# Every load of a decode kernel issued as two: even partitions from SyncE, odd partitions from ScalarE

## The chip, the core and the metric

The kernel runs on one core of a Trainium2 chip. A core has a matrix engine (TensorE, PE in the profile), VectorE (DVE), ScalarE (ACT), GpSimd (POOL) and SyncE (SP), each with its own instruction stream, and 16 DMA engines that move data between the device's memory (HBM) and the on-chip buffer (SBUF, 128 partitions). A load is issued by an instruction on SyncE or ScalarE and signals a semaphore when it has landed. The metric is the device time of the program in microseconds (us), lower is better. Before the change three runs took 219.29, 219.30 and 219.37 us, median 219.3.

## The reference

One decode step for a batch of 2: attention with 32 query heads over the last 4096 positions of a cache with 8 key/value heads, beside a dense layer with the Mish activation, mixed by a gate.

```python
# A: B=2, D=512, Hq=32, Hkv=8, Sk=32768, Dh=128; W=4096
q = (x @ wq).reshape(B, 1, Hq, Dh).transpose(0, 2, 1, 3)
k, v = the last W positions of the caches, each of 8 heads repeated 4 times
p = softmax(einsum("bhqd,bhkd->bhqk", q, k) * Dh ** -0.5)
a = einsum("bhqk,bhkd->bhqd", p, v)  ->  (B, 1, Hq * Dh) @ wo
# B: F=1792
h = x @ w1 + b1
b = (h * tanh(softplus(h))) @ w2
# gate
g = sigmoid((x * gate_w).sum(-1))
return g * a + (1 - g) * b
```

All of it is float32. The weights and the 4096 positions of both caches have to be read once: 91 MB.

## The kernel before, in words

The host lays the inputs out so that each load fills 128 partitions with long contiguous rows. There are three large buffers of 64 KB per partition (pool `stream`, `bufs=3`), and all large loads go through them in this order: `wq` (one piece of 1 MB, one of 7 MB), the caches of key/value heads 0 to 7 (`kv0` to `kv7`, 8 MB each, keys and values of one head side by side), `w12` (w1, the first heads' part of wo and the first seven row blocks of w2, 6.4 MB), `wo` (pieces of 5 MB and 2 MB), and last three pieces of w2 (1 MB, 0.5 MB, 0.25 MB), which go into the free end of `w12`'s buffer. A small load `sm` (13 KB: x, the gate's weights, b1) follows `wq`. All of them are issued by SyncE (`load`, line 64, and lines 70 and 294). A load into a buffer waits until TensorE has finished reading what was in it, so at most three large loads are held at once.

The compute follows the loads. `gates` and `queries` (lines 105 to 140) work from `sm` and `wq`. Then, for each key/value head, `scores` (line 148) multiplies the keys, VectorE finds the maximum (151), ScalarE takes the exponential with its sum (153, the tile `p`), `turned` transposes it on TensorE (160) and ScalarE copies that out (161, `pT`), and `values` multiplies by the values (172, the tile `o`). After every second head VectorE collects the diagonal blocks into `od` (179 to 182). For head 7 the common maximum of all heads and the factors that follow from it (`tops`, `factors`, `shares`) are woven in between. Then come `hidden` (line 235, the tile `hp`, and the Mish chain), `outputs` (224, the tile `ol`), the projection with wo and the first part of w2 (305, the tile `acc`), and the rest of w2 (315, the tile `fin`). A copy and a store end the program; before the store SyncE waits for the last eight loads to have landed (line 343).

The order within an engine is the order in which the scheduler of the language puts the instructions; `pin` keeps the pinned ones in the order written. The scheduler also gives each load one of eight semaphores in turn, and adds a wait to a load whose semaphore still belongs to an earlier load, so that this load goes only when the earlier one has landed. An engine that waits at an instruction does nothing that stands behind it.

Of the kernel before, what the change touches and what calls it, by code (L numbers as in the profile page):

```python
# [9 lines left out]
AF = mybir.ActivationFunctionType  # L10
# [3 lines left out]
P = 128  # L14
B = 2
D = 512
HQ = 32
HKV = 8
REP = HQ // HKV
# [4 lines left out]
BN = B * NH  # L24
NJ = 4
NT = 4
Q = 32
# [3 lines left out]
DC = D // P  # L31
FC = F // P
FG = 4
HALF = 4
CHUNK = 8192
# [4 lines left out]
CUTS = (0, 7, 11, 13, 14)  # L40
WO = (1, 6, 8)
ROWS = (24, 104)
WIDE = 2 * Q - B
AHEAD = DC * F + WO[0] * REP * D
# [3 lines left out]
def decode_kernel(ctx: ExitStack, tc: tile.TileContext, res, stored, small, wqh, wqt, kv_in, w12, wo, w2, out):  # L48
    nc = tc.nc
# [5 lines left out]
    ps_s = ctx.enter_context(tc.tile_pool(name="ps_s", bufs=2, space=bass.MemoryType.PSUM))  # L55
    ps_1 = ctx.enter_context(tc.tile_pool(name="ps_1", bufs=1, space=bass.MemoryType.PSUM))

    loads = []

    def load(name, *parts):  # L60
        t = stream.tile([P, 2 * CHUNK], F32, tag="s", name=name)
        x = 0
        for cols, src in parts:
            loads.append(nc.sync.dma_start(t[:, x : x + cols], src))  # L64
            x += cols
        return t

    wq_t = load("wq", (HEAD, wqh), (2 * CHUNK - HEAD, wqt))
    sm = const.tile([P, SMALL], F32, name="sm")
    loads.append(nc.sync.dma_start(sm, small))  # L70
    xT = sm[:, : DC * B].rearrange("p (c b) -> p c b", b=B)
    gw = sm[:, DC * B : DC * B + DC]
    b1 = sm[:, DC * B + DC :]
# [16 lines left out]
    x32 = const.tile([P, DC, Q], F32, name="x32")  # L90
    nc.gpsimd.memset(x32, 0.0)
    nc.gpsimd.tensor_copy(x32[:, :, ::RS], xT)  # L92
    qz = const.tile([P, HKV, BN * (Q + REP)], F32, name="qz")
# [13 lines left out]
    def gates():  # L107
        xg = const.tile([P, DC, B], F32, name="xg")
        nc.gpsimd.tensor_tensor(xg, xT, gw[:, :, None].to_broadcast([P, DC, B]), op=ALU.mult)
        zp = ps_1.tile([P, B], F32, tag="q", name="zp")  # L110
        for c in range(DC):
            nc.tensor.matmul(zp, ones, xg[:, c, :], start=(c == 0), stop=(c == DC - 1))  # L112
        g = const.tile([P, B], F32, name="g")
        omg = const.tile([P, B], F32, name="omg")
        nc.scalar.activation(g, zp, AF.Exp, scale=-1.0)
        nc.gpsimd.tensor_scalar_add(g, g, 1.0)  # L116
        nc.vector.reciprocal(g, g)  # L117
        nc.gpsimd.tensor_scalar(omg, g, -1.0, 1.0, op0=ALU.mult, op1=ALU.add)
        return g, omg
# [19 lines left out]
        for n in range(NH):  # L139
            nc.vector.tensor_copy(half[:, n], heads)  # L140

    pin = tc.keep_in_program_order

    def scores(kv, t):
        sc = ps_s.tile([P, 512], F32, tag="sc", name=f"sc{kv}")
        for m in range(BN):
            for j in range(NJ):
                nc.tensor.matmul(sc[Q * j : Q * j + Q, :], qz[:, kv, m * Q : m * Q + Q],  # L148
                                 t[:, (m * NJ + j) * 512 : (m * NJ + j + 1) * 512],
                                 start=(m == 0), stop=(m == BN - 1))  # L150
        nc.vector.tensor_reduce(mx[:, kv : kv + 1], sc, axis=AX.X, op=ALU.max, negate=True)  # L151
        p = work.tile([P, 512], F32, tag="p", name=f"p{kv}")
        nc.scalar.activation(p, sc, AF.Exp, bias=mx[:, kv : kv + 1], accum_out=ls[:, kv : kv + 1])  # L153
        return p

    def turned(kv, p):
        pp = ps_1.tile([P, NT, P], F32, tag="pt", name=f"pp{kv}")
        pT = single.tile([P, NT, P], F32, tag="pT", name=f"pT{kv}")
        for c in range(NT):
            pin(nc.tensor.transpose(pp[:, c, :], p[:, c * P : (c + 1) * P], ident))  # L160
        nc.scalar.copy(pT, pp)  # L161
        return pT

    pair = [None]
# [20 lines left out]
    def tops():  # L185
        mt = ps_1.tile([HKV, NJ, Q], F32, tag="q", name="mt")
        pin(nc.tensor.transpose(mt.rearrange("k j r -> k (j r)"), mx, ident))
        ms = const.tile([HKV, NJ, Q], F32, name="ms")
        nc.scalar.copy(ms, mt)
        m4 = ms.rearrange("k j (y n h) -> k j y n h", n=NH, h=REP)  # L190
        mj = const.tile([HKV, NJ, Q // NH // REP, REP], F32, name="mj")
        nc.vector.tensor_tensor(mj, m4[:, :, :, 0, :], m4[:, :, :, 1, :], op=ALU.min)
        top = const.tile([HKV, Q // NH // REP, REP], F32, name="top")
        nc.vector.tensor_reduce(top, mj.rearrange("k j y h -> k y h j"), axis=AX.X, op=ALU.min)  # L194
        for n in range(NH):
            nc.gpsimd.tensor_tensor(m4[:, :, :, n, :], m4[:, :, :, n, :],  # L196
                                    top[:, None].to_broadcast(mj.shape), op=ALU.subtract)
        nc.scalar.activation(ms, ms, AF.Exp, scale=-1.0)
        return ms

    def factors(ms):
# [27 lines left out]
    def hidden(t):  # L229
        w = t[:, : DC * F].rearrange("p (c f) -> p c f", c=DC)  # L230
        hp = ps_s.tile([P, FG * P], F32, tag="sc", name="hp")
        for c in range(DC):
            for j in range(NJ):
                n = min(FG, FC - j * FG) * P
                nc.tensor.matmul(hp[Q * j : Q * j + Q, :n], x32[:, c, :],  # L235
                                 w[:, c, j * FG * P : j * FG * P + n],
                                 start=(c == 0), stop=(c == DC - 1))
        hs = work.tile([P, FG * P], F32, tag="p", name="hs")
        nl = (FC - (NJ - 1) * FG) * P
        nc.scalar.copy(hs[:, :nl], hp[:, :nl])  # L240
        nc.scalar.copy(hs[: Q * (NJ - 1), nl:], hp[: Q * (NJ - 1), nl:])
        ht = ps_1.tile([P, FG, NJ, Q], F32, tag="pt", name="ht")

        def m(name):
            return const.tile([P, FC, B], F32, name=name)

        h, e, nu, de, ho = (m(x) for x in ("h", "e", "nu", "de", "ho"))
        for k in range(FG):
            nj = len(range(k, FC, FG))
            nc.tensor.transpose(ht[:, k, :nj, :].rearrange("p j r -> p (j r)"),  # L250
                                hs[: Q * nj, k * P : (k + 1) * P], ident[: Q * nj, : Q * nj])
        for j0, j1, nk in ((0, NJ - 1, FG), (NJ - 1, NJ, FC - (NJ - 1) * FG)):
            f0, f1 = j0 * FG, (j1 - 1) * FG + nk
            nc.vector.tensor_tensor(
                h[:, f0:f1, :].rearrange("p (j k) b -> p j k b", k=nk),
                ht[:, :nk, j0:j1, ::RS].rearrange("p k j b -> p j k b"),
                b1[:, f0:f1].rearrange("p (j k) -> p j k", k=nk)[:, :, :, None]
                .to_broadcast([P, j1 - j0, nk, B]), op=ALU.add)
        nc.gpsimd.tensor_scalar_min(e, h, CAP)
        nc.scalar.activation(e, e, AF.Exp)  # L260
        nc.gpsimd.tensor_tensor(ho, h, omg[:, None, :].to_broadcast([P, FC, B]), op=ALU.mult)
        nc.gpsimd.tensor_scalar_add(nu, e, 2.0)
        nc.gpsimd.tensor_tensor(nu, nu, e, op=ALU.mult)
        nc.gpsimd.tensor_scalar_add(de, nu, 2.0)
        nc.vector.reciprocal(de, de)
        nc.gpsimd.tensor_tensor(nu, nu, de, op=ALU.mult)
        nc.gpsimd.tensor_tensor(actT[:, :, ::RS], nu[:, : CUTS[1]], ho[:, : CUTS[1]], op=ALU.mult)
        nc.gpsimd.tensor_tensor(act2[:, :, Q - B : Q], nu[:, CUTS[1] :], ho[:, CUTS[1] :], op=ALU.mult)

    queries(0, wq_t[:, :CHUNK])  # L270
    queries(1, wq_t[:, CHUNK:])

    for kv in range(HKV):
        t = load(f"kv{kv}", (2 * CHUNK, kv_in[kv]))
        p = scores(kv, t[:, :CHUNK])
        ms = tops() if kv == HKV - 1 else None
        pT = turned(kv, p)
        values(kv, pT, t[:, CHUNK:], 0, 1)
        if kv == HKV - 1:
            kf, kl = factors(ms)  # L280
        values(kv, pT, t[:, CHUNK:], 1, 2)
        if kv == HKV - 1:
            r = shares(kl)
        values(kv, pT, t[:, CHUNK:], 2, NT)
    w12_t = load("w12", (AHEAD + CUTS[1] * D, w12))

    def flat(src, cuts, size):
        for f0, f1 in zip(cuts, cuts[1:]):
            yield (f1 - f0) * size, src[f0 * size * P : f1 * size * P].rearrange("(p x) -> p x", p=P)

    wo_t = load("wo", *flat(wo, [f - WO[0] for f in WO], REP * D))
    x = AHEAD + CUTS[1] * D
    for cols, src in flat(w2, [f - CUTS[1] for f in CUTS[1:]], D):
        loads.append(nc.sync.dma_start(w12_t[:, x : x + cols], src))
        x += cols
    hidden(w12_t)
    outputs(kf, r)

# [42 lines left out]
    output(3)  # L341

    landed = nc.sync.nop()
    for ld in loads[-8:]:
        tc.add_manual_dep(landed.ins, ld.ins.name,
                          mybir.DependencyInfo(mybir.DependencyClass.Sync, mybir.DependencyReason.DATA),
                          reason="SyncE sees the last loads land ahead of the store")
# [61 lines left out]
```

## Time and profile before

| | |
|---|---|
| median of three runs | 219.3 us |
| profiled execution: span, first to last instruction | 217.6 us |
| profiled execution's own time | not listed apart from its span; the runs' median is 1.7 us above it |
| bytes moved by DMA, mean rate over the span | 91.38 MB, 420 GB/s |
| busy: TensorE / VectorE / ScalarE / GpSimd | 113.0 / 21.5 / 15.5 / 8.0 us |
| mean granted TensorE clock | 0.867 |

In the profile, L with a number is a line of the kernel; an arrow (`sc<-kv,qz`) points from what is read to what is written; PEld is the weight load of TensorE; SPq and ACTq are instructions of the SyncE and ScalarE queues themselves, such as issues of loads. The time "to landing" of a load runs from its issue until its semaphore says it is complete, and so includes the time that it stood behind other loads. The granted clock is the share of full speed that the throttle gave TensorE.

### The profile page before, as it was taken

The page shows a single profiled execution, that of the slowest core. Times are in us where ns is not written, and L with a number is a line of the kernel's source. Part 1 is how long each engine was busy: PE and PEld are TensorE (multiplying, and loading weights), DVE is VectorE, ACT ScalarE, POOL GpSimd, SP SyncE. Part 2 cuts the span into 40 slices and gives each one's busy share as a digit, 9 for nine tenths or more (in the row PEclk, how much of TensorE's full clock was granted, in tenths as well). Part 3 has the DMA queues.
Part 4 walks back from the last instruction along what each step waited for, and adds up shares of the span by engine and source line. Part 5 has one row for each costly group of instructions (what it writes and reads, how often), then busy time and mean ns, then how long its engine had stood idle before and what let it go on. Part 6 is the DMA issues. An engine that isn't in the chain of part 4 may idle for free.

```text
span 217.6 us, 1836 instructions
## 1 busy us (share of the span) xinstructions
PE 113.0 (52%) x822; PEld 33.8 (16%) x822; DVE 21.5 (10%) x32; ACT 15.5 (7%) x34; POOL 8.0 (4%) x30
## 2 busy tenths in 40 slices
PE   0000798477046608543660754286075418758596
PEld 0000322112011102101110210012011001214123
DVE  0000000010001230100123010010501001251000
ACT  2000001111001100200110020002002000301001
POOL 8000000000000000000000000000000000102100
PEclk9999999979658985995998599769759967999979
DMA  9797988898899889989998999899989999989892
GB/s 361 337 506 337 581 385 385 385 569 385 385 398 566 385 376 446 518 385 398 446 497 385 410 434 506 385 422 422 497 385 434 410 432 452 452 364 482 375 404 113
DMA packets 2550, 91.38 MB, mean 420 GB/s; under 512 B 416, under 2 KB 496, under 8 KB 752
## 3 DMA queue, kind: packets, MB, share of 16 engines
q1 hardware_dynamic: 2544, 91.28, 97.3%
q8 instruction: 6, 0.10, 0.2%
HBM read 91.24 MB, written 0.04 MB: 419 GB/s over the span
## 4 chain that ended last, share of the span: by engine, by line
DMA 77%; PE 18%; ACT 2%; DVE 1%; SPq 1%; issue 0%; ACTq 0%
DMA kv<-in_kv 61%; DMA wo<-in_wo 16%; PE sc L148 7%; PE o L172 5%; PE acc L305 4%; ACT p L153 1%; DVE mx L151 1%; PE pp L160 1%; PE fin L315 1%; ACT pT L161 1%; SPq L64 0%; SPq L70 0%; DVE res L348 0%; ACTq L161 0%; ACTq L153 0%
## 5 line engine op out<-in xcount | busy, mean ns | idle before, releaser
L148 PE MATMUL sc<-kv,qz 128*32 128x512 f32 x256 | 44.1, 851 | 54.1 <-DMA kv<-in_kv 54.1
L172 PE MATMUL o<-kv,pT 128*32 128x512 f32 x256 | 29.5, 596 | 5.8 <-ACT pT L161 5.8
L128 PE MATMUL qp<-wq,x 128*32 128x512 f32 x64 | 12.1, 799 | 23.0 <-POOL x L92 23.0
L148 PEld LDWEIGHTS sc<-kv,qz 128*32 128x32 f32 x256 | 9.9, 150 | 87.6 <-DMA kv<-in_kv 60.7
L151 DVE TENSOR_REDUCE mx<-sc 128x1 f32<-128x512 f32 x8 | 5.5, 691 | 112.4 <-PE sc L148 112.4
L153 ACT ACTIVATE p<-sc,mx 128x512 f32<-128x512 f32 x8 | 5.5, 687 | 131.2 <-DVE mx L151 131.2
L160 PE MATMUL pp<-ident,p 128*128 128x128 f32 x32 | 5.3, 287 | 12.1 <-ACT p L153 12.1
L172 PEld LDWEIGHTS o<-kv,pT 128*32 128x32 f32 x256 | 7.3, 109 | 20.9 <-issue 13.1
L305 PE MATMUL acc<-wo,padded 128*32 128x512 f32 x56 | 7.9, 728 | 2.2 <-DMA wo<-in_wo 2.2
L182 DVE TENSOR_REDUCE od<-om 128x256 f32<-128x1024 f32 x4 | 7.6, 1900 | 0.1
L128 PEld LDWEIGHTS qp<-wq,x 128*32 128x32 f32 x64 | 2.5, 137 | 28.9 <-POOL x L92 23.0
L179 DVE TENSOR_TENSOR om<-o,pick 128x1024 f32<-128x1024 f32 x4 | 4.9, 1225 | 19.3 <-PE o L172 19.3
L196 POOL TENSOR_TENSOR ms<-ms,top 8x64 f32<-8x64 f32 x2 | 0.6, 309 | 159.0 <-DVE top L194 159.0
L160 PEld LDWEIGHTS pp<-ident,p 128*128 128x128 f32 x32 | 3.4, 140 | 18.6 <-ACT p L153 18.6
L161 ACT COPY pT<-pp 128x512 f32<-128x512 f32 x8 | 4.7, 585 | 6.2 <-PE pp L160 6.2
L235 PE MATMUL hp<-w,x 128*32 128x512 f32 (+1 forms) x32 | 3.6, 543 | 2.3 <-DMA w<-in_w 2.3
L305 PEld LDWEIGHTS acc<-wo,padded 128*32 128x32 f32 x56 | 2.1, 129 | 8.0 <-issue 4.9
L305 PE MATMUL acc<-w,padded 128*32 128x512 f32 x22 | 2.8, 601 | 0.4 <-DVE padded L226 0.4
L117 DVE RECIPROCAL g<-g 128x2 f32<-128x2 f32 x1 | 0.2, 166 | 22.4 <-POOL g L116 22.4
L134 PE MATMUL qt<-ident,qs 128*128 128x128 f32 x8 | 1.3, 287 | 1.4 <-ACT qs L131 1.4
L112 PEld LDWEIGHTS zp<-xg,ones 128*128 128x128 f32 x8 | 1.8, 327 | 1.7 <-issue 1.7
L131 ACT ACTIVATE qs<-qp 128x512 f32<-128x512 f32 x2 | 1.2, 597 | 10.6 <-PE qp L128 10.6
(65 smaller groups left out, 31.3 us busy)
## 6 DMA issues: line engine op xcount, KB each, us to landing
wq<-in_wqt SPq DMA_DIRECT2D x1, 7168.0 KB, 21.4
w<-in_w SPq DMA_DIRECT2D x1, 6400.0 KB, 41.1
wo<-in_wo SPq DMA_DIRECT2D x1, 5120.0 KB, 34.8
wo<-in_wo SPq DMA_DIRECT2D x1, 2048.0 KB, 39.3
wq<-in_wqh SPq DMA_DIRECT2D x1, 1024.0 KB, 4.9
w<-in_w SPq DMA_DIRECT2D x1, 1024.0 KB, 41.3
w<-in_w SPq DMA_DIRECT2D x1, 512.0 KB, 42.0
w<-in_w SPq DMA_DIRECT2D x1, 256.0 KB, 42.1
```

What stands on the lines that cost most here:

```text
L128: nc.tensor.matmul(qp[Q * k : Q * k + Q, :], x32[:, c, :], w[:, c, k, :], start=(c == 0), stop=(c == DC - 1))
L148: nc.tensor.matmul(sc[Q * j : Q * j + Q, :], qz[:, kv, m * Q : m * Q + Q], t[:, (m * NJ + j) * 512 : (m * NJ + j + 1) * 512], start=(m == ...
L151: nc.vector.tensor_reduce(mx[:, kv : kv + 1], sc, axis=AX.X, op=ALU.max, negate=True)
L153: nc.scalar.activation(p, sc, AF.Exp, bias=mx[:, kv : kv + 1], accum_out=ls[:, kv : kv + 1])
L160: pin(nc.tensor.transpose(pp[:, c, :], p[:, c * P : (c + 1) * P], ident))
L161: nc.scalar.copy(pT, pp)
L172: pin(nc.tensor.matmul(o[Q * j : Q * j + Q], pT[:, c, Q * j : Q * j + Q], t[:, (c * NJ + j) * 512 : (c * NJ + j + 1) * 512], start=(c == 0 ...
L179: nc.vector.tensor_tensor(ov, pair[0].rearrange("p k (m d) -> p k m d", m=BN), pick[:, None, :, None].to_broadcast([P, 2, BN, DH]), op=ALU ...
L182: nc.vector.tensor_reduce(od[:, kv - 1 : kv + 1], ov.rearrange("p k m d -> p k d m"), axis=AX.X, op=ALU.add)
L235: nc.tensor.matmul(hp[Q * j : Q * j + Q, :n], x32[:, c, :], w[:, c, j * FG * P : j * FG * P + n], start=(c == 0), stop=(c == DC - 1))
L305: return nc.tensor.matmul(acc[Q * j : Q * j + Q, :], lhsT, rhs, start=(n_col[j] == 1), stop=(n_col[j] == n))
L315: nc.tensor.matmul(fin[Q * j : Q * j + Q, :], lhsT[:, y : y + Q], rhs[:, j * P : (j + 1) * P], start=(done[0] == 0), stop=(done[0] == n_fi ...
```

## The change

Each load becomes two: a new helper `both` issues the even partitions of the destination (`dst[0::2]`) from SyncE and the odd ones (`dst[1::2]`) from ScalarE. The small load `sm` stays whole on SyncE. Because ScalarE's stream now holds loads as well as arithmetic, the issues are written out at the places where they shall stand: heads 0 and 1 right after `wq` and `sm`, head 2 after the queries, then the load for head `kv + 3` after the values of head `kv`, `w12` after head 5, and `wo` with the three pieces of w2 after head 6. The issues, ScalarE's arithmetic and two groups of matmuls are pinned in that order. The exponential of `tops` moves from its function to the place behind `turned`. SyncE's wait before the store covers the last 16 loads in place of 8.

```diff
+    def both(dst, src):
+        for queue, y in ((nc.sync, 0), (nc.scalar, 1)):
+            loads.append(pin(queue.dma_start(dst[y::2], src[y::2])))
 
     def load(name, *parts):
         t = stream.tile([P, 2 * CHUNK], F32, tag="s", name=name)
         x = 0
         for cols, src in parts:
-            loads.append(nc.sync.dma_start(t[:, x : x + cols], src))
+            both(t[:, x : x + cols], src)
             x += cols
         return t
 
     wq_t = load("wq", (HEAD, wqh), (2 * CHUNK - HEAD, wqt))
     sm = const.tile([P, SMALL], F32, name="sm")
     loads.append(nc.sync.dma_start(sm, small))
+
+    def head(kv):
+        return load(f"kv{kv}", (2 * CHUNK, kv_in[kv]))
+
+    ahead = [head(kv) for kv in range(2)]
...
-        nc.scalar.activation(ms, ms, AF.Exp, scale=-1.0)
         return ms
...
     queries(0, wq_t[:, :CHUNK])
     queries(1, wq_t[:, CHUNK:])
+    ahead.append(head(2))
 
     for kv in range(HKV):
-        t = load(f"kv{kv}", (2 * CHUNK, kv_in[kv]))
+        t = ahead[kv]
         p = scores(kv, t[:, :CHUNK])
         ms = tops() if kv == HKV - 1 else None
         pT = turned(kv, p)
+        if kv == HKV - 1:
+            pin(nc.scalar.activation(ms, ms, AF.Exp, scale=-1.0))
         values(kv, pT, t[:, CHUNK:], 0, 1)
...
-    w12_t = load("w12", (AHEAD + CUTS[1] * D, w12))
...
-    wo_t = load("wo", *flat(wo, [f - WO[0] for f in WO], REP * D))
-    x = AHEAD + CUTS[1] * D
-    for cols, src in flat(w2, [f - CUTS[1] for f in CUTS[1:]], D):
-        loads.append(nc.sync.dma_start(w12_t[:, x : x + cols], src))
-        x += cols
+        if kv < HKV - 3:
+            ahead.append(head(kv + 3))
+        elif kv == HKV - 3:
+            w12_t = load("w12", (AHEAD + CUTS[1] * D, w12))
+        elif kv == HKV - 2:
+            wo_t = load("wo", *flat(wo, [f - WO[0] for f in WO], REP * D))
+            x = AHEAD + CUTS[1] * D
+            for cols, src in flat(w2, [f - CUTS[1] for f in CUTS[1:]], D):
+                both(w12_t[:, x : x + cols], src)
+                x += cols
     hidden(w12_t)
...
-    for ld in loads[-8:]:
+    for ld in loads[-16:]:
```

More of the change, by code (lines that the diff above doesn't have):

```diff
@@ L56, in decode_kernel @@
     ps_1 = ctx.enter_context(tc.tile_pool(name="ps_1", bufs=1, space=bass.MemoryType.PSUM))
+    pin = tc.keep_in_program_order
     loads = []
+    def both(dst, src):
+        for queue, y in ((nc.sync, 0), (nc.scalar, 1)):
+            loads.append(pin(queue.dma_start(dst[y::2], src[y::2])))
     def load(name, *parts):
@@ L114, in gates @@
         omg = const.tile([P, B], F32, name="omg")
-        nc.scalar.activation(g, zp, AF.Exp, scale=-1.0)
+        pin(nc.scalar.activation(g, zp, AF.Exp, scale=-1.0))
         nc.gpsimd.tensor_scalar_add(g, g, 1.0)
@@ L140, in queries @@
             nc.vector.tensor_copy(half[:, n], heads)
-    pin = tc.keep_in_program_order
     def scores(kv, t):
@@ L147, in scores @@
             for j in range(NJ):
-                nc.tensor.matmul(sc[Q * j : Q * j + Q, :], qz[:, kv, m * Q : m * Q + Q],
-                                 t[:, (m * NJ + j) * 512 : (m * NJ + j + 1) * 512],
-                                 start=(m == 0), stop=(m == BN - 1))
+                pin(nc.tensor.matmul(sc[Q * j : Q * j + Q, :], qz[:, kv, m * Q : m * Q + Q],
+                                     t[:, (m * NJ + j) * 512 : (m * NJ + j + 1) * 512],
+                                     start=(m == 0), stop=(m == BN - 1)))
         nc.vector.tensor_reduce(mx[:, kv : kv + 1], sc, axis=AX.X, op=ALU.max, negate=True)
         p = work.tile([P, 512], F32, tag="p", name=f"p{kv}")
-        nc.scalar.activation(p, sc, AF.Exp, bias=mx[:, kv : kv + 1], accum_out=ls[:, kv : kv + 1])
+        pin(nc.scalar.activation(p, sc, AF.Exp, bias=mx[:, kv : kv + 1], accum_out=ls[:, kv : kv + 1]))
         return p
@@ L160, in turned @@
             pin(nc.tensor.transpose(pp[:, c, :], p[:, c * P : (c + 1) * P], ident))
-        nc.scalar.copy(pT, pp)
+        pin(nc.scalar.copy(pT, pp))
         return pT
@@ L188, in tops @@
         ms = const.tile([HKV, NJ, Q], F32, name="ms")
-        nc.scalar.copy(ms, mt)
+        pin(nc.scalar.copy(ms, mt))
         m4 = ms.rearrange("k j (y n h) -> k j y n h", n=NH, h=REP)
@@ L234, in hidden @@
                 n = min(FG, FC - j * FG) * P
-                nc.tensor.matmul(hp[Q * j : Q * j + Q, :n], x32[:, c, :],
-                                 w[:, c, j * FG * P : j * FG * P + n],
-                                 start=(c == 0), stop=(c == DC - 1))
+                pin(nc.tensor.matmul(hp[Q * j : Q * j + Q, :n], x32[:, c, :],
+                                     w[:, c, j * FG * P : j * FG * P + n],
+                                     start=(c == 0), stop=(c == DC - 1)))
         hs = work.tile([P, FG * P], F32, tag="p", name="hs")
         nl = (FC - (NJ - 1) * FG) * P
-        nc.scalar.copy(hs[:, :nl], hp[:, :nl])
+        pin(nc.scalar.copy(hs[:, :nl], hp[:, :nl]))
         nc.scalar.copy(hs[: Q * (NJ - 1), nl:], hp[: Q * (NJ - 1), nl:])
@@ L268, in hidden, with flat @@
         nc.gpsimd.tensor_tensor(act2[:, :, Q - B : Q], nu[:, CUTS[1] :], ho[:, CUTS[1] :], op=ALU.mult)
+    def flat(src, cuts, size):
+        for f0, f1 in zip(cuts, cuts[1:]):
+            yield (f1 - f0) * size, src[f0 * size * P : f1 * size * P].rearrange("(p x) -> p x", p=P)
     queries(0, wq_t[:, :CHUNK])
     queries(1, wq_t[:, CHUNK:])
+    ahead.append(head(2))
     for kv in range(HKV):
-        t = load(f"kv{kv}", (2 * CHUNK, kv_in[kv]))
+        t = ahead[kv]
         p = scores(kv, t[:, :CHUNK])
@@ L284, in decode_kernel @@
         values(kv, pT, t[:, CHUNK:], 2, NT)
-    w12_t = load("w12", (AHEAD + CUTS[1] * D, w12))
-    def flat(src, cuts, size):
-        for f0, f1 in zip(cuts, cuts[1:]):
-            yield (f1 - f0) * size, src[f0 * size * P : f1 * size * P].rearrange("(p x) -> p x", p=P)
-    wo_t = load("wo", *flat(wo, [f - WO[0] for f in WO], REP * D))
-    x = AHEAD + CUTS[1] * D
-    for cols, src in flat(w2, [f - CUTS[1] for f in CUTS[1:]], D):
-        loads.append(nc.sync.dma_start(w12_t[:, x : x + cols], src))
-        x += cols
+        if kv < HKV - 3:
[8 more added lines that the diff above has]
+                x += cols
     hidden(w12_t)
```

## The prediction

> **What bounds the kernel now.** I read the page first: the span, the DMA queue's share, the chain that ended last, and the loads' times from issue to landing.
>
> ```profile
> span 217.6 us, 1836 instructions
> q1 hardware_dynamic: 2544, 91.28, 97.3%
> DMA 77%; PE 18%; ACT 2%; DVE 1%; SPq 1%; issue 0%; ACTq 0%
> w<-in_w SPq DMA_DIRECT2D x1, 6400.0 KB, 41.1
> wo<-in_wo SPq DMA_DIRECT2D x1, 5120.0 KB, 34.8
> wo<-in_wo SPq DMA_DIRECT2D x1, 2048.0 KB, 39.3
> wq<-in_wqh SPq DMA_DIRECT2D x1, 1024.0 KB, 4.9
> w<-in_w SPq DMA_DIRECT2D x1, 256.0 KB, 42.1
> sm<-in_small SPq DMA_DIRECT2D x1, 13.0 KB, 21.1
> ```
>
> One queue, SyncE's, is busy for 97.3% of the span on all 16 DMA engines: 211.7 us for 91.28 MB, or 431 GB/s. The rest is the start and the end: the first load (1,024 KB, 2.4 us at that rate) lands at 0.72 + 4.9 = 5.6, so bytes flow from about 3.2 us, and the 256 KB piece that is last lands at about 215.0. Between these there is nothing to fill. Next, the end of the trace in order of time, which shows what hangs on the last loads (columns: start, length, engine, line, output<-inputs, count, idle time before it and what ended that).
>
> ```profile
> 171.11 0.82 SPq L64 DMA_DIRECT2D wo<-in_wo  x2
> 171.97 1.43 SPq L294 DMA_DIRECT2D w<-in_w  x3
> 178.69 5.58 PE L148 MATMUL sc<-kv,qz 128*32 128x512 f32 x32 [7.65 <-DMA kv<-in_kv]
> 185.08 0.69 ACT L153 ACTIVATE p<-sc,mx 128x512 f32<-128x512 f32 x1 [17.73 <-DVE mx L151]
> 185.91 0.66 PE L160 MATMUL pp<-ident,p 128*128 128x128 f32 x4 [0.54 <-ACT p L153]
> 189.81 1.92 PE L172 MATMUL o<-kv,pT 128*32 128x512 f32 x16
> 193.06 1.95 DVE L182 TENSOR_REDUCE od<-om 128x256 f32<-128x1024 f32 x1
> 194.08 3.63 PE L235 MATMUL hp<-w,x 128*32 128x512 f32 x32 [2.35 <-DMA w<-in_w]
> 198.70 1.88 PE L224 MATMUL ol<-kf,od 128*128 128x8 f32 x16
> 201.01 2.81 PE L305 MATMUL acc<-w,padded 128*32 128x512 f32 x22 [0.43 <-DVE padded L226]
> 206.00 7.91 PE L305 MATMUL acc<-wo,padded 128*32 128x512 f32 x56 [2.18 <-DMA wo<-in_wo]
> 214.86 0.84 PE L315 MATMUL fin<-w,padded 128*32 128x128 f32 x24
> 216.09 0.36 SPq L349 DMA_DIRECT2D out<-res  x1
> ```
>
> The last head's softmax (p, ScalarE) starts at 185.08, as soon as its scores exist. What follows on TensorE (o, hp, ol, acc) waits for data only twice, 2.35 us for w12 and 2.18 us for the first piece of wo, which lands at 171.11 + 34.8 = 206.0. So that softmax has about 4.5 us of slack and no more. SyncE issues the last five loads between 171.1 and 173.4, far ahead, and blocks nobody.
>
> **The change, part by part.** *Bytes.* The same 91.28 MB; each 64 KB row stays one row. 16 loads become 32, and 16 of these move to ScalarE's queue, as 16 issues. On SyncE a kv issue took 0.33 us (median), the pieces of w2 1.43 / 3 = 0.48 us. ScalarE has room for the early ones:
>
> ```profile
> 0.71 1.28 ACT L115 ACT_TABLE_LOAD   x1 [0.71 <-PEq L394]
> 26.76 0.17 ACT L115 ACTIVATE g<-zp 128x2 f32<-128x2 f32 x1 [24.76 <-PE zp L112]
> ACT p L153 <- DVE mx L151: 131.2, 8, 18.8
> SPq L64 <- PE o L172: 85.5, 7, 12.8
> ```
>
> Four issues (about 1.6 us) now go ahead of the table load, which is needed at 26.8: nothing, behind 23 us of cover. The loads of kv2 to kv7, w12 and wo wait on both queues for TensorE to leave the buffer, as SyncE does now (85.5 us, seven times). Behind that wait on ScalarE stands the softmax of the next head, whose own wait (131.2 us over eight) ends later, since its scores follow those values on TensorE: nothing. The pins leave TensorE's, VectorE's and GpSimd's order as it was in the built program; ScalarE's arithmetic too.
>
> *The small load.* sm stays on SyncE, behind half of wq.
>
> ```profile
> 22.76 0.20 POOL L92 COPY x<-sm 128x8 f32<-128x8 f32 x1 [17.70 <-DMA sm<-in_small]
> 38.16 0.60 ACT L131 ACTIVATE qs<-qp 128x512 f32<-128x512 f32 x1 [4.35 <-PE qp L128]
> 62.77 5.52 PE L148 MATMUL sc<-kv,qz 128*32 128x512 f32 x32 [8.76 <-DMA kv<-in_kv]
> ```
>
> Its 8 rows per engine may now take turns with ScalarE's 64 KB rows. One such row takes 2.4 us at 431/16 GB/s, so sm may be up to 8 x 2.4 = 19.5 us late. Queries then end at 57.6 instead of 38.1, where kv2's load is issued; kv0 and kv1 keep the engines busy until about 62.7. That covers it, just; with the cover gone, each us beyond is paid in full (I allow 0 to 3). ScalarE's ring may come out of it up to two rows ahead, which would bring its share of wo up to 4.9 us earlier. I take 0.
>
> *The new wait.* In the built program every load signals one of eight semaphores in turn, and one is reused only when its previous load has landed. Before, the last loads took semaphores long free. With twice as many loads the turn comes round sooner. ScalarE's own order near the end reads:
>
> ```
> wo (first piece)    waits: kv6 landed and read (its buffer)
> wo (second piece)
> w2 (2048 columns)   waits: ScalarE's half of kv7 landed
> w2 (1024 columns)   waits: ScalarE's half of w12 landed
> w2 (512 columns)    waits: ScalarE's half of wo's first piece landed
> p7 = softmax of the last head
> ms, pT7, ms exp, hs, hs, e, asum
> ```
>
> The last head's softmax is queued behind an issue that cannot go before wo's first piece is in: 206.0, against 185.08 when it ran before. SyncE has the same waits, with only the store behind them; the pieces of w2 still join queues that hold data (wo's second piece and the larger pieces of w2, 8 us of it, follow 206.0), so the stream ends at 215.0 as before.
>
> The sum: landing 206.0, plus 0.5 for the held issue and its hand-over: p7 starts at 206.5. From p7 to the end the trace of before takes 217.6 − 185.08 = 32.5 us, of which 2.35 (w12) and 2.18 (wo) were waits for loads that will long be in: 28.0 us. Between them nothing else binds: od, ready at 195.0 after p7 at 185.08, leads ol by 3.7 us, and hp moves 2.35 earlier only. End: 234.5. One size is not in these rows: TensorE's clock.
>
> ```profile
> 178.60:182.70 4.10, 4.00 (x20) 0.99 (x24) 0.00 (x0) 0.00 (x0) 0.00 (x0) 0.51 1.07 462
> 182.70:192.00 9.30, 6.94 (x56) 1.91 (x48) 2.35 (x7) 1.81 (x5) 0.88 (x3) 1.00 0.95 411
> 207.20:210.30 3.10, 3.10 (x21) 0.87 (x17) 0.00 (x0) 0.00 (x0) 0.00 (x0) 0.55 1.00 423
> ```
>
> (Windows; the third column from the end is the granted clock.) After an idle stretch it was 0.51 for 4 us, and o ran at 1.00 only because the scores had just used that up. Now TensorE idles some 22 us ahead of pp and o, so they may get the slow 4 us: at most 2 us more; the slow 3.1 us inside acc may go: at most 1.4 us less. I take +1: span 235.5. The runs' median is 219.3 against this execution's span of 217.6 (its own time is not listed apart), so 1.7 lies around it: **237 us**. Its own range: 231 (ScalarE's ring two rows ahead, slow clock not paid) to 243 (sm's 3 us, the clock's second us, and a stream 1% slower).
>
> **The rivals.** *Half-height loads stream slower.* Every load in this trace covers 128 partitions; how 64 alternate ones are shared over 16 engines, and whether two such loads add up, no row shows. Bounds: at 431 GB/s nothing; if the engines reach half of it, the 202.8 us of stream until wo's first piece (3.2 to 206.0) become 405.6. With a factor f the time is 3.2 + 202.8/f + 31.2 (0.5, 28.0, 1 and 1.7): 248 at 0.95, 257 at 0.9, 349 at 0.65, 440 at 0.5. For it: the engines work in step, as the page's row of GB/s by slice shows (slices of 506 to 581 beside ones of 337 to 398, where the mean is 420), so that a clash of two on one destination would recur in every row.
>
> ```profile
> GB/s 361 337 506 337 581 385 385 385 569 385 385 398 566 385 376 446 518 385 398 446 497 385 410 434 506 385 422 422 497 385 434 410 432 452 452 364 482 375 404 113
> ```
>
> Against: each queue's half still touches every group of neighbouring partitions, and all rows are as long as before. The nearest row is the full rate; so I keep 1.
>
> The Trainium skill, page "SBUF — State Buffer", section "Can I just issue two DMAs to hit both halves?", says that two concurrent loads on the two halves of the partitions were only 6% faster than one, and its table gives 196 GB/s for 64 partitions against 328 for 128: an estimate of f = 0.63 from that page, 356 us. Its halves were contiguous and these are interleaved; no run here shows it.
>
> *One ring is served first (not slower).* If the engines took ScalarE's ring ahead of SyncE's, its half of wo could land ahead of SyncE's halves of w12 and wo and a part of kv7: 3.3 + 2.6 + 1.6 MB, or 17 us, earlier, at 188.6. p7 may start at 185.08 + 4.5 = 189.6 at no cost, so from a landing at 189.1 on the hold is free, and the end is set by the stream: 219.3, or 218.9 with the start 0.4 us earlier because wq's larger piece need not wait for the issue of the small one. For it: nothing in a trace with one queue. Against: both rings hold equal rows, issued at the same moments.
>
> *In between*: a ring ahead by three to six rows, 220 to 230.
>
> **How the numbers follow.** The hold at full rate: 0.64, 231 to 243. Slower streaming: 0.28, spread over 245 to 440. ScalarE's ring far ahead: 0.04, half of it faster by over 0.2% (0.4 us, about what a measurement of this kernel can tell from no change), half within it. In between: 0.04. Left out of 230 to 360 are the streams under f = 0.62 (0.12), the free hold (0.04), most of the in-between (0.03): 0.19. Faster by streaming better than 431 GB/s with no hold gets 0.01; so faster 0.03, same 0.02, slower 0.95.
>
> **What would show it.** ScalarE's queue waits about 20 us at the last w2 issue for wo, behind kv7's scores; p7 starts within 1 us of the landing of wo's first ScalarE half; that idle time stands before pp on TensorE; the DMA's share falls to nothing about 20 us before the end; 2,800 packets on two queues (2,544 and 16 for each of 16 added loads). sm lands up to 19.5 us later and the first scores start later with no trace of it after kv3. Wrong would be: p7 at 185 with the hold absent; wo's first piece landing well after 206 (slower stream); or a gap of the DMA near 60 us, which sm would have caused.

## The result and the profile after

| | before | changed |
|---|---|---|
| median | 219.3 us | 235.74 us |
| lowest to highest of four runs | 219.21 to 219.37 | 233.84 to 237.26 |
| ratio, 95% interval | | 1.0743 (1.0688 to 1.0798) |
| span of the profiled execution | 217.6 us | 232.0 us |
| its own time | not listed | 233.84 us |
| mean granted TensorE clock | 0.867 | 0.868 |

The change made the kernel 7.4% slower; 237 was forecast, within 230 to 360. The bytes are the same and they stream as fast as before. From the page of the changed kernel: the span, the row of DMA busy tenths over 40 slices, and the two queues with their packets, MB and share of the engines' time.

```profile
span 232.0 us, 1877 instructions
DMA  9899898998989989899898999988999999998000
q1 hardware_dynamic: 1520, 45.67, 45.9%
q10 hardware_dynamic: 1280, 45.61, 45.5%
```

The two queues together carry 2,800 packets, each of them half of the bytes, and are busy for 91.4% of 232.0 us, or 212.0 us against 211.7 before. The DMA engines are busy until the last three slices, some 17 us, and then idle: the end is no longer set by the stream. Its end in order of time, from the timeline of the changed kernel:

```profile
177.38 1.38 ACTq L63 DMA_DIRECT2D wo<-in_wo  x2
178.80 24.80 ACTq L63 DMA_DIRECT2D w<-in_w  x3
182.87 5.51 PE L156 MATMUL sc<-kv,qz 128*32 128x512 f32 x32 [5.55 <-DMA kv<-in_kv]
188.44 0.69 DVE L159 TENSOR_REDUCE mx<-sc 128x1 f32<-128x512 f32 x1 [17.02 <-PE sc L156]
203.65 0.69 ACT L161 ACTIVATE p<-sc,mx 128x512 f32<-128x512 f32 x1 [30.03 <-DMA wo<-in_wo]
204.48 1.12 PE L168 MATMUL pp<-ident,p 128*128 128x128 f32 x4 [15.03 <-ACT p L161]
206.33 1.94 PE L180 MATMUL o<-kv,pT 128*32 128x512 f32 x8 [0.73 <-ACT pT L169]
210.76 1.92 PE L180 MATMUL o<-kv,pT 128*32 128x512 f32 x16
212.50 3.61 PE L242 MATMUL hp<-w,x 128*32 128x512 f32 x32
219.41 2.38 PE L318 MATMUL acc<-w,padded 128*32 128x512 f32 x19 [0.42 <-DVE padded L233]
221.65 6.14 PE L318 MATMUL acc<-wo,padded 128*32 128x512 f32 x52
230.40 0.37 SPq L362 DMA_DIRECT2D out<-res  x1
```

The maximum of the last head's scores is ready at 189.1 (188.44 + 0.69). ScalarE begins its exponential at 203.65, and its idle time is put down to the load of wo, which the exponential does not read. What stands between is the row of the three w2 issues: the last of them leaves at 203.1 and ends at 203.6. TensorE waits 15.03 us for that exponential, and after it nothing on TensorE waits for a load any more.

### The profile page after: what moved, and what is told of

Same layout as the page of the kernel before. It is cut to its first block, busy times and chain, and to the rows that moved or that the text cites. A ratio compares the mean times of both kernels' runs of the same rounds, so it can differ in the third digit from the quotient of the medians.

```text
span 232.0 us, 1877 instructions
## 1 busy us (share of the span) xinstructions
PE 110.6 (48%) x822; PEld 34.5 (15%) x822; DVE 21.5 (9%) x32; ACT 15.4 (7%) x34; POOL 8.0 (3%) x30
## 4 chain that ended last, share of the span: by engine, by line
DMA 64%; PE 29%; ACT 3%; DVE 1%; issue 1%; SPq 0%; ACTq 0%; POOL 0%; DVEq 0%
DMA kv<-in_kv 37%; DMA sm<-in_small 16%; DMA wo<-in_wo 11%; PE o L180 7%; PE sc L156 7%; PE qp L138 5%; PE acc L318 4%; PE hp L242 1%; ACT p L161 1%; PE pp L168 1%; ACT pT L169 1%; DVE mx L159 1%; PE fin L328 1%; PE zp L122 1%; PE ol L231 1%
## 5 line engine op out<-in xcount | busy, mean ns | idle before, releaser
L156 PE MATMUL sc<-kv,qz 128*32 128x512 f32 x256 | 41.3, 802 | 43.9 <-DMA kv<-in_kv 43.9
L180 PE MATMUL o<-kv,pT 128*32 128x512 f32 x256 | 32.8, 651 | 5.8 <-ACT pT L169 5.8
L138 PE MATMUL qp<-wq,x 128*32 128x512 f32 x64 | 10.7, 711 | 40.0 <-POOL x L102 40.0
L180 PEld LDWEIGHTS o<-kv,pT 128*32 128x32 f32 x256 | 7.6, 115 | 22.4 <-issue 14.5
L318 PE MATMUL acc<-wo,padded 128*32 128x512 f32 x56 | 7.0, 593 | 0.0
L328 PE MATMUL fin<-w,padded 128*32 128x128 f32 x56 | 2.3, 273 | 0.0
```

The lines of the kernel that those rows point to most:

```text
L138: nc.tensor.matmul(qp[Q * k : Q * k + Q, :], x32[:, c, :], w[:, c, k, :], start=(c == 0), stop=(c == DC - 1))
L156: pin(nc.tensor.matmul(sc[Q * j : Q * j + Q, :], qz[:, kv, m * Q : m * Q + Q], t[:, (m * NJ + j) * 512 : (m * NJ + j + 1) * 512], start=(m ...
L180: pin(nc.tensor.matmul(o[Q * j : Q * j + Q], pT[:, c, Q * j : Q * j + Q], t[:, (c * NJ + j) * 512 : (c * NJ + j + 1) * 512], start=(c == 0 ...
L318: return nc.tensor.matmul(acc[Q * j : Q * j + Q, :], lhsT, rhs, start=(n_col[j] == 1), stop=(n_col[j] == n))
L328: nc.tensor.matmul(fin[Q * j : Q * j + Q, :], lhsT[:, y : y + Q], rhs[:, j * P : (j + 1) * P], start=(done[0] == 0), stop=(done[0] == n_fi ...
```

## The experiments

**1. The pieces of w2 whole, on SyncE.** This takes the three last issues off ScalarE and leaves every other load split.

```diff
-                both(w12_t[:, x : x + cols], src)
+                loads.append(pin(nc.sync.dma_start(w12_t[:, x : x + cols], src)))
...
-    for ld in loads[-16:]:
+    for ld in loads[-13:]:
```

> The three pieces of w2 are issued whole by SyncE; all other loads stay split over the two queues. If the added time is ScalarE held at the last w2 issue: the last head's softmax starts within 1 us of its scores (near 189 us) in place of 203.7, and the time falls back to 219.3 to 221.5 us; the part above 219.3 would be SyncE's ring landing its halves 1 to 4 us after ScalarE's. If the halves themselves stream slower, or the late small load is paid for: 230 us or more.

Measured: 220.12 us, ratio to before 1.0029 (1.0017 to 1.0040). Timeline of this version:

```profile
182.75 3.64 PE L156 MATMUL sc<-kv,qz 128*32 128x512 f32 x32 [3.47 <-DMA kv<-in_kv]
187.18 0.69 ACT L161 ACTIVATE p<-sc,mx 128x512 f32<-128x512 f32 x1 [13.15 <-DVE mx L159]
197.09 5.33 PE L242 MATMUL hp<-w,x 128*32 128x512 f32 x32 [3.26 <-DMA w<-in_w]
207.95 6.14 PE L318 MATMUL acc<-wo,padded 128*32 128x512 f32 x52
```

The exponential follows its maximum at once, TensorE waits for w12 again, and all but 0.6 of the 16 us are gone with 26 of the 32 half loads still there.

**2. All loads split, ScalarE's w2 issues written further down.** The first goes behind the exponential of `tops`, the other two behind the Mish exponential.

```diff
+    late = []
+
+    def odd(n):
+        for _ in range(n):
+            loads.append(pin(nc.scalar.dma_start(*late.pop(0))))
...
-        nc.scalar.activation(e, e, AF.Exp)
+        pin(nc.scalar.activation(e, e, AF.Exp))
+        odd(2)
...
             pin(nc.scalar.activation(ms, ms, AF.Exp, scale=-1.0))
+            odd(1)
...
-                both(w12_t[:, x : x + cols], src)
+                loads.append(pin(nc.sync.dma_start(w12_t[0::2, x : x + cols], src[0::2])))
+                late.append((w12_t[1::2, x : x + cols], src[1::2]))
```

`odd` issues the next loads of `late` on ScalarE, whose second copy of `hs` is pinned as well.

> Every load stays split; only ScalarE's three w2 issues are written further down in its order, the first behind the last head's softmax, the other two behind the Mish exponential. Held ScalarE: 219.3 to 221.5 us, with ScalarE's waits for wo now standing where it has nothing to do. Splitting as such (more loads, more semaphore waits, slower stream): as the changed kernel, 234 to 237 us.

Measured: 220.28 us, ratio 1.0062 (1.0018 to 1.0107); five of the six runs lie between 219.92 and 220.58 us, and one at 223.03 widens the interval. Timeline:

```profile
189.03 0.69 ACT L167 ACTIVATE p<-sc,mx 128x512 f32<-128x512 f32 x1 [15.50 <-DVE mx L165]
203.23 4.71 ACTq L85 DMA_DIRECT2D w<-in_w  x2
207.96 6.30 PE L327 MATMUL acc<-wo,padded 128*32 128x512 f32 x55
214.34 0.58 ACT L353 COPY asum<-acc 128x512 f32<-128x512 f32 x1 [11.48 <-DMA w<-in_w]
```

The last two issues, and with them the waits for wo, now end at 207.9, and the next thing that ScalarE has to do is a copy at 214.3, which needs the sums of TensorE that end then (207.96 + 6.30 = 214.26; the line of the copy names a load, but ScalarE's issues were done at 207.9). The same copy started at 213.98 before the change. Same loads, same number of semaphores, another place in one engine's order: the whole loss but about 1 us is gone.

**3. Both halves on SyncE.**

```diff
-        for queue, y in ((nc.sync, 0), (nc.scalar, 1)):
+        for queue, y in ((nc.sync, 0), (nc.sync, 1)):
```

> Both halves of every load go on SyncE's queue, one after the other: as many loads and as many waits for a reused semaphore as in the changed kernel, but none of them on ScalarE. Held ScalarE: 218.9 to 220.5 us. If half-height loads are slower by themselves: the stream until wo's first piece, 203 us, grows in proportion, 222 us at 1% slower and 240 us at 10%.

Measured: 220.73 us, ratio 1.0058 (1.0043 to 1.0073), 0.2 us above the range: half-height loads cost some 1.2 us when they run one after another, and not 16. Timeline:

```profile
175.57 32.23 SPq L63 DMA_DIRECT2D w<-in_w  x6
187.10 0.69 ACT L161 ACTIVATE p<-sc,mx 128x512 f32<-128x512 f32 x1 [17.71 <-DVE mx L159]
```

The six issues of w2 halves are drawn out over 32 us, up to 207.8, since they wait for the same landings; but they stand on SyncE, and the exponential runs at 187.10.

**4. A smaller dose: two pieces of w2 in place of three.** The last w2 issue on ScalarE then waits for its half of w12, not of wo.

```diff
-CUTS = (0, 7, 11, 13, 14)
+CUTS = (0, 7, 11, 14)
...
     output(2)
-    output(3)
...
-    for ld in loads[-16:]:
+    for ld in loads[-14:]:
```

> The changed kernel with the last two pieces of w2 joined, so two pieces in place of three, split over both queues like the rest. The last w2 issue on ScalarE then reuses the semaphore of w12's half (landed near 190 us) in place of that of wo's half (203.1). Held ScalarE: the last head's softmax starts near 191 us, 12 to 13 us earlier, and the time is 219.5 to 222 us. If it is the number of w2 issues or halves on ScalarE and not what the last one waits for: about 230 us (two issues in place of three).

Measured: 223.47 us, ratio 1.0206 (1.0180 to 1.0232). Timeline:

```profile
180.48 12.00 ACTq L63 DMA_DIRECT2D w<-in_w  x2
192.53 0.69 ACT L161 ACTIVATE p<-sc,mx 128x512 f32<-128x512 f32 x1 [18.70 <-DMA w<-in_w]
193.36 1.12 PE L168 MATMUL pp<-ident,p 128*128 128x128 f32 x4 [4.15 <-ACT p L161]
195.21 1.94 PE L180 MATMUL o<-kv,pT 128*32 128x512 f32 x8 [0.73 <-ACT pT L169]
216.70 0.38 PE L328 MATMUL fin<-w,padded 128*32 128x128 f32 x2
```

Removing one of three issues took the median from 235.74 to 223.47, three quarters of the loss: what counts is which landing the last issue waits for (192.0 here, 203.1 there: 11.1 us apart, and the spans 232.0 and 221.4 are 10.6 apart). The time is 1.5 us above the expected range. I had the softmax at 191, where it came at 192.53, and did not price the clock: behind 4.15 us of idle TensorE, pp and the first eight of o ran at about half speed (1.12 and 1.94 us). The kernel before took 0.66 and, for the same eight of o, 1.07:

```profile
187.30 1.07 PE L172 MATMUL o<-kv,pT 128*32 128x512 f32 x8 [0.73 <-ACT pT L161]
```

How much idle time it takes is not settled by these runs: in experiment 1 the scores took 3.64 us behind 3.47 us of idle, and hp 5.33 us (3.63 before the change) behind 3.26 us.

**5. The small load first.**

```diff
+    sm = const.tile([P, SMALL], F32, name="sm")
+    loads.append(pin(nc.sync.dma_start(sm, small)))
     wq_t = load("wq", (HEAD, wqh), (2 * CHUNK - HEAD, wqt))
-    sm = const.tile([P, SMALL], F32, name="sm")
-    loads.append(nc.sync.dma_start(sm, small))
```

> The changed kernel with the small load issued first, ahead of wq. It then lands within 4 us in place of 39.8. If its lateness cost nothing and only set ScalarE's ring ahead: the first scores start near 42 us, both halves of wo's first piece land together near 206 us, the softmax of the last head starts up to 3 us later than the 203.7 of the changed kernel's profile, and the time is 235.7 to 239 us, the same or slower. If the late small load was paid for at the end: up to 17 us faster, below 232 us.

Measured: 238.05 us, ratio 1.0867 (1.0806 to 1.0928), slower than the changed kernel. The dma view gives, for each half, its size and the time from issue to landing; first the changed kernel, with the issue of the small load from its timeline:

```profile
1.94 0.58 SPq L75 DMA_DIRECT2D sm<-in_small  x1
wo<-in_wo SPq DMA_DIRECT2D x1, 2560.0 KB, 30.0
wo<-in_wo ACTq DMA_DIRECT2D x1, 2560.0 KB, 25.7
sm<-in_small SPq DMA_DIRECT2D x1, 13.0 KB, 37.8
```

then this version, with the exponential in its timeline:

```profile
wo<-in_wo SPq DMA_DIRECT2D x1, 2560.0 KB, 31.6
wo<-in_wo ACTq DMA_DIRECT2D x1, 2560.0 KB, 31.4
sm<-in_small SPq DMA_DIRECT2D x1, 13.0 KB, 1.7
207.15 0.69 ACT L161 ACTIVATE p<-sc,mx 128x512 f32<-128x512 f32 x1 [37.27 <-DMA wo<-in_wo]
```

In the changed kernel the small load landed at 1.94 + 37.8 = 39.7 us, 17.0 us later than before, and ScalarE's half of wo landed 4.3 us ahead of SyncE's (203.1 and 207.4, both issued at 177.38). With the small load out of the way the halves land together, 206.6 and 206.8, and the hold ends 3.5 us later (207.15 against 203.65; the spans are 235.4 and 232.0 us). The late small load cost nothing that these runs can tell (experiment 6 against experiment 1), and by putting SyncE's ring behind it even let the hold end sooner.

**6. No hold and level rings.** The edits of experiments 1 and 5 together.

> w2 whole on SyncE and the small load first; everything else split over two queues. Nothing holds ScalarE and the rings stay level. If the 0.6 to 1 us left in w2_whole is the ring that lags: 219.0 to 219.8 us, the same as the kernel before. If it is the cost of split loads: 220.1 or more.

Measured: 219.87 us, ratio 1.0027 (1.0016 to 1.0037), between the two values expected, and no different from experiment 1 (1.0029). So the lag of one ring is not what is left. In this timeline wo is there at 206.26 against 206.00 before:

```profile
206.26 7.91 PE L318 MATMUL acc<-wo,padded 128*32 128x512 f32 x56 [2.13 <-DMA wo<-in_wo]
```

**7. The order alone.** The changed kernel's order and pins, every load whole and on SyncE.

```diff
-        for queue, y in ((nc.sync, 0), (nc.scalar, 1)):
-            loads.append(pin(queue.dma_start(dst[y::2], src[y::2])))
+        loads.append(pin(nc.sync.dma_start(dst, src)))
...
-    for ld in loads[-16:]:
+    for ld in loads[-8:]:
```

> The changed kernel's order, pins and places of the issues, but every load whole and on SyncE. If the split alone made the difference: 219.0 to 219.7 us, as the kernel before. If the new order or the pins cost something: the 0.6 us left in the versions whose softmax is not held, or more.

Measured: 219.45 us, ratio 0.9998 (0.9987 to 1.0009). The order and the pins are free; the 0.3% left in experiments 1 and 6 belongs to the split, with its second queue.

**8. Neighbouring partitions in place of alternate ones.**

```diff
-            loads.append(pin(queue.dma_start(dst[y::2], src[y::2])))
+            h = slice(y * P // 2, (y + 1) * P // 2)
+            loads.append(pin(queue.dma_start(dst[h], src[h])))
```

> The changed kernel with partitions 0 to 63 on SyncE and 64 to 127 on ScalarE, in place of even and odd. If two half-height loads share the engines at the full rate whatever partitions they take: 234 to 239 us as the changed kernel. If the rule of the Trainium skill's page SBUF holds here (two concurrent loads on the two halves 6% faster than one): the stream runs at some 0.63 of its rate and the time is about 356 us.

Measured: 439.42 us, ratio 2.0037 (2.0007 to 2.0067). The windows view of this version (length; busy times of the engines; granted clock, DMA share, GB/s):

```profile
100.00:200.00 100.00, 27.25 (x176) 7.29 (x180) 5.18 (x5) 4.09 (x9) 0.00 (x0) 0.64 1.00 210
300.00:400.00 100.00, 25.15 (x169) 6.72 (x169) 5.18 (x5) 2.73 (x6) 0.00 (x0) 0.65 0.99 210
```

The DMA engines are as busy as before, at 210 GB/s in place of 431: 0.49 of the rate, with nothing but the choice of partitions changed. The Trainium skill, page "SBUF — State Buffer", section "Can I just issue two DMAs to hit both halves?", says that two concurrent loads on the two halves are hardly faster than one. This holds here: 439.42 us on two queues, and 448.53 with the same halves one after the other on one (experiment 9). My estimate of 0.63 was too mild: the 196 and 328 GB/s of that page's table are for loads of 1 MiB, and its last column, the limit for large loads, has about 218 GB/s for 64 partitions and 436 for 128, a half, which agrees with the 0.49 measured. The same rule does not carry over to alternate partitions, which ran at the full rate in the changed kernel.

**9. The neighbouring halves on one queue.** As 8, both on SyncE.

> Partitions 0 to 63 and 64 to 127 as two loads, both on SyncE, one after the other. If a load of 64 neighbouring partitions is served at half the rate by itself: 435 to 442 us, as with two queues. If it was the two queues getting in each other's way: 219 to 222 us, as even and odd partitions did on one queue.

Measured: 448.53 us in two runs, ratio 2.0436 (2.0372 to 2.0500), 6.5 us above the range, and on the side of the shape: a load of 64 neighbouring partitions is slow by itself, with one queue as with two. Why the second queue is worth 9 us in that state was not followed further.

## Why the prediction was right

*The hold.* Shown. Experiments 1 and 2 take it away in two ways, 3 puts it on an engine where nothing waits behind it, and 4 and 5 make it end sooner and later; the span follows by what the softmax moves (11.1 us sooner and 10.6 less, 3.5 later and 3.4 more).

*The sum.* In the profiled execution: landing 203.1, issue and hand-over 0.55, and 28.35 from the softmax to the end, together 232.0. Predicted were 206.0, 0.5 and 29.0, together 235.5. The first term was mis-sized: I named a lead of ScalarE's ring of up to 4.9 us and took 0; it was 2.9 us against the landing before, and experiment 5 shows that the small load makes it. The profiled execution is the fastest of the four, 233.84 us, and for it the sum is 3.5 us too high; that the median of 235.74 lies within 1.3 us of 237 is in part luck. The four runs reach from 233.84 to 237.26, more than before the change; why they spread was not tried.

*The clock.* The two parts were there, with other sizes: from the softmax to the end of o it took 9.0 us (203.65 to 212.68) where it took 6.65 before (185.08 to 191.73), 2.4 more at the slow clock; the two acc groups, with no wait between them, took about 8.8 us in place of 2.81 + 7.91, 1.9 less. Both are beyond the bounds that I gave (2 and 1.4), and they nearly cancel: from the softmax to the end it is 0.4 more than the 28.0 without the clock; I took 1.

*Costs set at nothing.* The 17.0 us of the small load lie inside the 19.5 allowed, and the first scores came at 55.05 in place of 42.01; by the second head TensorE waited for loads again (2.22 us at 67.58):

```profile
39.80 0.20 POOL L102 COPY x<-sm 128x8 f32<-128x8 f32 x1 [34.74 <-DMA sm<-in_small]
55.05 3.64 PE L156 MATMUL sc<-kv,qz 128*32 128x512 f32 x32
67.58 3.64 PE L156 MATMUL sc<-kv,qz 128*32 128x512 f32 x32 [2.22 <-DMA kv<-in_kv]
```

The order and the pins were free (experiment 7), and ScalarE's early issues lie within the 0.3% of experiment 6. The length of the hold was 14.5 us past its scores and not 20, because the scores also came later (182.87, on SyncE's half of kv7, in place of 178.69) and wo's half earlier.

*The rivals.* Slower streaming did not come with alternate partitions, but it is real: with neighbouring halves it is the whole 0.5 that I had as the bound. The reason given against it, that each half still touches every group of neighbouring partitions, fits both results; the runs do not show how rows are shared over engines, so it stays a reading. Two of the times given for slower streams are 3 us off: by their own formula 0.9 gives 260 and 0.65 gives 346. ScalarE's ring was ahead in small, 4.3 us against the 17 that would have cleared the hold, but no engine served it first: with the small load out of the way the halves land together (experiment 5).

## What to carry to other kernels

An issue of a load on an engine that also computes is a place where that engine can stop, and the wait need not be for anything near it: here it was a semaphore used eight loads earlier, reached because there were twice as many loads. Before moving issues to such an engine, list for each one what it waits for and what stands behind it, above all the last ones, which are issued far ahead of time. Here the one queue was busy for 97% of the span, and the second won nothing in any version.

## What the runs showed of the hardware that was not expected

Two half-height loads cost 0.3% when they take alternate partitions and a factor of 2.00 when they take neighbouring ones (219.87 in experiment 6 and 439.42 us with 219.31 beside them), and the second is so on one queue too (448.53).

A 13 KB load in one queue beside 64 KB rows in the other landed 17.0 us later, which is about seven of the eight rows of 2.43 us (64 KB at 431/16 GB/s) with which I had let it take turns; issued first, it landed in 1.7 us. No version tried was faster than the kernel before.
